# FNet mixing gated by a GLU: other places in the list of units, and an end in smaller pieces

## The chip, the cores and the metric

The kernel runs on one core of a Trainium2 chip. The time is the device time of one execution in microseconds (us); several executions are timed and their median is given. One further execution is recorded by the profiler, and everything that is read from a view of the profile comes from that one. The engines are TensorE (PE, matmuls), VectorE (DVE), ScalarE (ACT), GpSimd (POOL, which here only issues DMAs) and SyncE (SP, which issues loads and the last stores).

## The reference

x has 2048 rows and 512 columns; all matrices are float32.

```python
xn = layernorm(x)                                  # no scale, no offset
a, b = xn @ dft_hid_re.T, xn @ dft_hid_im.T        # DFT over the hidden dimension
s = dft_seq_re @ a - dft_seq_im @ b                # DFT over the sequence, real part
h = sigmoid(xn @ w_gate) * (xn @ w_up)             # GLU
g = silu(h @ w_down)
out = x + s * g
```

## The kernel before, in words

**Precision.** Each float32 operand is split into two parts by `split` (L70 to L73): a ScalarE copy rounded to the matmul's type (L72, "hi") and a VectorE subtraction that keeps the rest (L73, "lo"). `mm3` (L75 to L78) makes three matmuls of each product: hi by hi (L76), hi by lo (L77), lo by hi (L78). So the first matmul of a product needs only the copy, and the second the subtraction too.

**Fewer products.** All large products use a scheme of seven block products (numbered 1 to 7 in the code) instead of eight. Their operands are sums and differences of blocks, made by `combine` (L126 to L128) on VectorE; the results are put together from PSUM by copies on ScalarE (`snap`) and additions on VectorE (`plus`, `join`, `give`). The sequence DFT also uses its symmetry, which leaves some small products, here called inner products (letters a to g in a plan).

**Storage.** Working memory is a pool of pages of 512 KB. Which page a tile gets is settled when the program is built: one that is free by then in program order. The instruction that takes it waits on the chip until the page's last reader is done, and that reader can be a store. Partial results go to DRAM and come back: `g_part` (GLU output, L312, accumulated by the DMA), `f_part` (sequence DFT, L831), `s_part` (sums of xn, L647), `w_part` (differences of the hidden DFT's weights, L678), `i_part` (the inner products' operands, already split, `keep` in `inner_a`, L744). `put_x` copies x to the output (L979), onto which the gated blocks are accumulated at the end (L1032).

**The list of units.** A unit is one group of matmuls of some products and the operands that they need; `units` holds 251 of them, in this order:

- 0 to 90: thirteen GLU blocks of seven units, 18 matmuls each (4.1 us). Each takes one "down" product of an earlier block along (bank pd), whose result `gather` (L310 copies, L312 accumulate) brings out.
- 91 to 223: the sequence products of four chunks, 12 matmuls each (2.7 us). The order within a chunk is a string in `PLAN`: a digit is one of the four quarters of that block product, a letter an inner product (6 matmuls). The last down products (6 matmuls) are put in after so many digits (`LEFT`).
- 224 to 250: the hidden DFT, in two halves (pairs) of the output; the last unit is cut (`run_last`).

There is no scheduler. Before unit n the loop below emits what was registered for it by `sooner`, the loads of five units ahead and the splits of two units ahead (three, where n is in `deep`); then the matmuls; then what was registered by `after`. The engines work strictly in this order, so an instruction that waits holds back all behind it on its engine.

```python
for f in early.get(n, []):                                   # sooner(n, f)
    f()
for k in range(n, min(n + LOAD_AHEAD + 1, len(units))):      # loads, SP
    ...
for k in range(n, min(n + SPLIT_AHEAD + 1 + (n in deep), len(units))):   # splits, ACT and DVE
    ...
run()                                                        # matmuls, then copies out of PSUM
for f in extra.get(n, []):                                   # after(n, f)
    f()
```

The places are numbers in tables: `DEEP` (units with one more split ahead), `AL` (first operands made so many units early), a fixed 3 and 4 for the sums of a chunk and of the inner products, `SI`, `SL` and `GL` (silu, sums and splits of the hidden DFT), and a list for each of the inner operands, the weight differences and the copies of x.

Of the kernel before, what the change touches and what calls it, by code (L numbers as in the profile page):

```python
# [34 lines left out]
def fnet_glu_kernel(ctx: ExitStack, tc: tile.TileContext, x, x_t, c_re, c_im, w_h, w_gu, w_down, out):  # L35
# [285 lines left out]
    LEFT = 2,4,6,8,10,12,14  # L321
    HEAD = {(1, 0): "g", (1, 1): "g n u0", (2, 0): "u2", (2, 1): "p1 d0 d1 u1 r", (3, 0): "p3 x1 g d2 u3", (3, 1): "X5 g x2"}
    S0 = 7, 10, 11, 12
    H0 = 8, 12, 13, 14
    L4 = 9, 11, 14, 17
    S4 = 7,8,10,11
# [105 lines left out]
    def block(h, w, made, before, job, late):  # L432
# [3 lines left out]
        if not made:  # L436
            for i, v in zip((-3, 0, 1, 3), w["s"]):
                sooner(n + i, v.get)
# [255 lines left out]
    def a_operands():  # L694
# [11 lines left out]
        "1111 5555 6666 aa 3333 7777 bb 4444",  # L706
        "1e1e1f1f 5c5c55 66663g3g 7777 3d3d 4444",
        "11115555 6666aa7777bb4444 3e3e3f3f",
        "cc1g1g1d1d 5555 6666 33 7777 33 4444",
    )  # L710
    LETTER = "aabb"
    DEEP = {(c, k, 3) for c in range(2) for k in (1, 5, 6, 7, 4)}
    AL = {(0,4,0):4,(0,4,2):4,(0,7,0):4,(0,7,2):4,(0,3,0):4,(0,3,2):4}
# [68 lines left out]
    class Chunk:  # L782
# [102 lines left out]
    class Inner:  # L885
# [30 lines left out]
        def step(self, k):  # L916
            i, m = self.count[k], len(units)
            self.count[k] += 1
            if ("t", k, i) in self.b:
                v = self.b["t", k, i]  # L920
                sooner(m - 7, v.load)
                sooner(m - 4, v.get)
# [3 lines left out]
    def seq_units(job, c_sums):  # L926
# [4 lines left out]
        for q in range(2):  # L931
            sooner(n - 9 + 4 * q, ops[1, q].load)
            sooner(n - 5 + 4 * q, ops[1, q].get)
        inner_a([n + i for i in (-43,-41,-38,-36,-34,-31,-27,-24,-20,-6,-3)])
# [20 lines left out]
        sums_ahead(diffs, blocks, w_part, range(starts[2] + 5, starts[2] + 9), 4)  # L955


    def hidden_units():
# [4 lines left out]
        WH = {1: n - 11, 5: n - 8, 6: n - 5}  # L963
# [7 lines left out]
        LAST = NT // 2 - 1, 4  # L971
# [16 lines left out]
        SI = {(0,2):8,(0,7):9,(0,3):10}  # L988
        SL = {(0,6,0):4,(0,6,1):5,(0,7,0):5,(0,7,1):6}
        GL = {(0,5,0):3,(0,5,1):3,(0,6,0):3,(0,6,1):3,(0,2,0):3,(0,2,1):3,(0,7,0):3}  # L990
        for pair in range(NT // 2):
# [16 lines left out]
            for i, k in enumerate(TURNED):  # L1008
                if k in BLOCK and (pair, k) != LAST:
                    after(n - 88 + 4 * (i + 2 * pair), lambda pair=pair, k=k: put_x(pair, *BLOCK[k]))  # L1010
# [7 lines left out]
            def done(k, pair=pair, gl=gl, ps=ps, s=s, begin_chain=begin_chain):  # L1018
# [5 lines left out]
                def give(ch, name=None, op=None, swap=False):  # L1024
                    g = gl[BLOCK[k]].get()
                    r = s[name] if name else page([2, SB], F32)
                    for d in range(2):
                        a, b = r[:, d, :] if name else g[:, d, :], ps[ch, d]
                        nc.vector.tensor_tensor(r[:, d, :], *((b, a) if swap else (a, b)), op=op or ALU.mult)
                    if name:  # L1030
                        nc.vector.tensor_mul(r, r, g)
                    nc.gpsimd.dma_start(place_out(pair, *BLOCK[k]), r, accum_op=ADD)  # L1032
# [175 lines left out]
```

## Time and profile before

| what | before |
|---|---|
| median of 3 executions | 804.94 us (804.63 to 805.74) |
| the profiled execution | 803.52 us, of which the span is 801.7 us |
| matmuls, busy TensorE | 3588, 793.1 us |
| VectorE busy | 709.1 us, 928 instructions |
| ScalarE busy | 540.9 us |
| granted TensorE clock | 1.00 |

The span is what the profiler records from the first to the last instruction or transfer; 1.8 us of the execution lie around it. A matmul's end is modelled: one of 128x512 is shown with 0.39 us, while the next begins 0.23 us after it, so what TensorE loses is read from the starts of its matmuls and not from its busy time. A line such as "L72 ACT ACTIVATE page<-page" names the source line, the engine, the operation, and what is written and read, without the numbers of the buffers. What stands in brackets at a row's end is how long the engine was idle before it, and what ended that.

### The profile page before, as it was taken

The numbers are of one execution on the slowest core, as the hardware profiler recorded it, in microseconds if no ns is written. First come the engines' busy times: TensorE is split into PE (matmuls) and PEld (weight loads), VectorE is DVE, ScalarE is ACT, GpSimd is POOL, SyncE is SP. The second block draws the span as 40 slices with busy tenths as digits, with TensorE's granted clock in tenths as the row PEclk, the third lists the DMA queues.
The fourth block names the chain that finished last, engine by engine and source line by source line (L and its number), as shares of the span: only waits on it lengthen the run. The fifth ranks groups of instructions, "written<-read, shape, count | busy, mean of one in ns | idle before, by whom it ended". The sixth has DMA issues, their size and how long they took to land.

```text
span 801.7 us, 10262 instructions
## 1 busy us (share of the span) xinstructions
PE 793.1 (99%) x3588; PEld 656.1 (82%) x3588; DVE 709.1 (88%) x928; ACT 540.9 (67%) x840; POOL 122.0 (15%) x168
## 2 busy tenths in 40 slices
PE   9999999999999999999999999999999999999997
PEld 8988888888888888788888888788887888888886
DVE  7999889889998989988998897899698899888986
ACT  4688887888877878777977755553544645548371
POOL 2004351211221212121110000001010000000201
PEclk9999999999999999999999999999999999999999
DMA  7048799886986899987997797629977584874826
GB/s 282 35 158 209 175 222 207 210 159 106 182 206 217 218 232 261 252 204 149 243 325 221 194 346 229 210 80 331 410 264 260 200 303 185 301 269 164 206 57 106
DMA packets 49556, 172.13 MB, mean 215 GB/s; under 512 B 5472, under 2 KB 5728, under 8 KB 49504
## 3 DMA queue, kind: packets, MB, share of 16 engines
q0 software_dynamic: 20112, 69.75, 40.0%
q1 hardware_dynamic: 29312, 101.66, 36.0%
q8 instruction: 28, 0.46, 0.2%
q14 instruction: 24, 0.20, 0.1%
q10 hardware_dynamic: 80, 0.07, 0.0%
HBM read 104.86 MB, written 70.26 MB: 218 GB/s over the span
## 4 chain that ended last, share of the span: by engine, by line
PE 91%; issue 3%; DMA 3%; DVE 2%; ACT 0%; POOL 0%; ACTq 0%; DVEq 0%; POOLq 0%
PE pd L78 5%; PE pd L76 5%; PE pd L77 5%; PE ga L76 5%; PE ga L77 5%; PE ga L78 5%; PE ua L77 5%; PE ua L78 5%; PE ua L76 5%; PE gb L77 4%; PE gb L78 4%; PE gb L76 4%; PE gc L77 3%; PE gc L78 3%; PE ub L76 3%; PE uc L76 3%
## 5 line engine op out<-in xcount | busy, mean ns | idle before, releaser
L73 DVE TENSOR_TENSOR page<-page 128x1024 fp32r<-128x1024 f32 (+2 forms) x408 | 374.4, 944 | 64.1 <-ACT page L72 63.3
L72 ACT ACTIVATE page<-page 128x1024 fp32r<-128x1024 f32 (+2 forms) x408 | 319.1, 834 | 121.8 <-DVE page L128 109.8
L128 DVE TENSOR_TENSOR page<-page 128x512 f32<-128x512 f32 (+2 forms) x280 | 224.0, 819 | 1.2 <-DMA page<-in_w_gu_dram 0.3
L310 ACT ACTIVATE page<-pd 128x512 f32<-128x512 f32 x140 | 82.3, 600 | 44.5 <-PE pd L78 39.5
L312 POOL DMA_DIRECT2D g_part<-page x76 | 65.0, 855 | 277.0 <-ACT page L310 265.6
L76 PE MATMUL ga<-page 128*128 128x512 f32 x200 | 78.1, 390 | 0.5 <-ACT page L443 0.5
L77 PE MATMUL ga<-page 128*128 128x512 f32 x200 | 78.0, 390 | 0.0
L78 PE MATMUL pd<-page 128*128 128x512 f32 x200 | 77.9, 390 | 0.0
L78 PE MATMUL ga<-page 128*128 128x512 f32 x200 | 77.8, 389 | 0.0
L76 PE MATMUL pd<-page 128*128 128x512 f32 x200 | 77.8, 389 | 0.0
L77 PE MATMUL pd<-page 128*128 128x512 f32 x200 | 77.8, 389 | 0.0
L77 PE MATMUL ua<-page 128*128 128x512 f32 x196 | 76.4, 390 | 0.1
L76 PE MATMUL ua<-page 128*128 128x512 f32 x196 | 76.3, 389 | 0.0
L78 PE MATMUL ua<-page 128*128 128x512 f32 x196 | 76.3, 389 | 0.0
L77 PE MATMUL gb<-page 128*128 128x512 f32 (+1 forms) x140 | 53.8, 385 | 0.1
L78 PE MATMUL gb<-page 128*128 128x512 f32 (+1 forms) x140 | 53.6, 383 | 0.0
L76 PE MATMUL gb<-page 128*128 128x512 f32 (+1 forms) x140 | 53.6, 383 | 0.0
L77 PE MATMUL ub<-page 128*128 128x512 f32 x132 | 51.5, 390 | 0.0
L76 PE MATMUL ub<-page 128*128 128x512 f32 x132 | 51.4, 389 | 0.0
L78 PE MATMUL ub<-page 128*128 128x512 f32 x132 | 51.3, 389 | 0.0
L77 PE MATMUL gc<-page 128*128 128x512 f32 x124 | 48.9, 395 | 0.6 <-DVE page L73 0.5
L78 PE MATMUL gc<-page 128*128 128x512 f32 x124 | 48.4, 391 | 0.1
(154 smaller groups left out, 1296.1 us busy)
## 6 DMA issues: line engine op xcount, KB each, us to landing
g_part<-page POOLq DMA_DIRECT2D x84, 512.0 KB, 6.6
page<-in_c_re_dram SPq DMA_DIRECT2D x49, 512.0 KB, 5.2
page<-in_c_im_dram SPq DMA_DIRECT2D x33, 512.0 KB, 6.3
page<-in_w_gu_dram SPq DMA_DIRECT2D x26, 512.0 KB, 6.0
f_part<-page POOLq DMA_DIRECT2D x16, 512.0 KB, 4.9
page<-f_part SPq DMA_DIRECT2D x16, 512.0 KB, 3.7
page<-i_part SPq DMA_DIRECT2D x14, 512.0 KB, 4.2
page<-in_w_down_dram SPq DMA_DIRECT2D x13, 512.0 KB, 4.8
```

Source lines behind the costliest of these rows:

```text
L72: nc.scalar.activation(hi, src, AF.Copy)
L73: nc.vector.tensor_tensor(lo, src, hi.bitcast(F32), op=SUB)
L76: nc.tensor.matmul(ps, ws[0], ms[0], start=first, stop=False, skip_group_check=go_on)
L77: nc.tensor.matmul(ps, ws[0], ms[1], start=False, stop=False, skip_group_check=go_on)
L78: nc.tensor.matmul(ps, ws[1], ms[0], start=False, stop=last, skip_group_check=go_on)
L128: (engine or nc.vector).tensor_tensor(dst, a, b, op=op)
L310: nc.scalar.activation(pg[:, o, :], po, AF.Copy, scale=float(sign))
L312: nc.gpsimd.dma_start(g_part[i], pg, accum_op=ADD)
```

## The change

Nothing is computed in another way; the same products are made. Four things move, and the end is cut differently.

1. **Order of products.** Four strings of `PLAN` place the inner products (and a few quarters) elsewhere among the quarters, and `LEFT` brings the last two down products of a chunk one quarter earlier.
2. **Splits and sums of the chunks.** `DEEP` names other units. Two new tables, `CSUM` and `ISUM`, give the lead of single sums instead of the fixed 3 and 4 units. `AL` makes some first operands 3 to 6 units early.
3. **Other operands.** The inner operands (`inner_a`, sums, splits and their stores by POOL), the weight differences (units 164, 170, 173 and 178 instead of 167 to 170), the sums of xn and x, the silu calls, sums and splits of the hidden DFT, the copies of x by POOL, and the operands of the GLU blocks (`S0`, `H0`, `L4`, `S4`, `w["s"]`) get other places.
4. **The end.** The last but one block of output is gated and accumulated in two halves of 256 KB instead of one of 512 KB. The last unit makes its two halves in pieces of 256, 320, 256 and 192 columns instead of 256, 512 and 256; the final store, on two queues, is 192 columns wide instead of 256.

```diff
-    LEFT = 2,4,6,8,10,12,14
+    LEFT = 2, 4, 6, 8, 10, 11, 13
...
-        "1e1e1f1f 5c5c55 66663g3g 7777 3d3d 4444",
+        "11ee1f15fc5c5566663gg377773d3d4444",
...
-    DEEP = {(c, k, 3) for c in range(2) for k in (1, 5, 6, 7, 4)}
+    DEEP = {(0, 1, 3), (0, 5, 3), (0, 6, 3), (0, 7, 3), (0, 4, 3), (1, 1, 3), (1, 5, 3), (1, 7, 3), (1, 4, 3), (3, 6, 3), (2, 4, 0), (2, 6, 3), (3, 4, 1), (3, 7, 3), (0, 7, 1), (3, 7, 0), (2, 7, 2), (0, 6, 0)}
+    CSUM = {(0, 7, 1): 5, (2, 6, 0): 4, (2, 6, 1): 5, (1, 6, 0): 2, (3, 4, 2): 3, (1, 5, 1): 5, (2, 6, 3): 3}
...
                 v = self.sums[k, pp]
-                sooner(m - 6, v.load)
-                sooner(m - 3, v.get)
+                lead = CSUM.get((self.tc, k, pp), 3)
+                sooner(m - lead - 3, v.load)
+                sooner(m - lead, v.get)
...
-        inner_a([n + i for i in (-43,-41,-38,-36,-34,-31,-27,-24,-20,-6,-3)])
+        inner_a([n + i for i in (-45, -38, -37, -36, -34, -31, -27, -24, -16, -10, -4)])
...
-        sums_ahead(diffs, blocks, w_part, range(starts[2] + 5, starts[2] + 9), 4)
+        sums_ahead(diffs, blocks, w_part, [starts[2] + i for i in (2, 8, 11, 16)], 4)
...
                 def give(ch, name=None, op=None, swap=False):
                     g = gl[BLOCK[k]].get()
                     r = s[name] if name else page([2, SB], F32)
+                    halves = (pair, k) == (LAST[0], 3)
                     for d in range(2):
                         a, b = r[:, d, :] if name else g[:, d, :], ps[ch, d]
                         nc.vector.tensor_tensor(r[:, d, :], *((b, a) if swap else (a, b)), op=op or ALU.mult)
+                        if halves:
+                            nc.vector.tensor_mul(r[:, d, :], r[:, d, :], g[:, d, :])
+                            nc.gpsimd.dma_start(place_out(pair, *BLOCK[k])[:, d, :], r[:, d, :], accum_op=ADD)
+                    if halves:
+                        return
...
-                for d, at in ((0, slice(0, SB // 2)), (1, slice(0, SB)), (0, slice(SB // 2, SB))):
+                for d, at in ((0, slice(0, SB // 2)), (1, slice(0, CUT)), (0, slice(SB // 2, SB)), (1, slice(CUT, SB))):
```

(`CUT` is 320. Line numbers after the change are 2 to 11 higher than before: L807, L814 and L824 become L809, L816 and L826, and L744 becomes L746.)

How this moves single instructions is shown at three places. First POOL near the end of the GLU blocks, at unit 71 to 78; each row is one DMA, written tensor and read page. Before:

```order
L312 DMA g_part5_91<-page_3316 128x1024
L744 DMA i_part_96<-page_3324 128x1024
L312 DMA g_part7_93<-page_3360 128x1024
L312 DMA g_part6_92<-page_3400 128x1024
L312 DMA g_part4_90<-page_3472 128x1024
```

And after:

```order
L312 DMA g_part5_91<-page_3316 128x1024
L312 DMA g_part7_93<-page_3355 128x1024
L312 DMA g_part6_92<-page_3393 128x1024
L312 DMA g_part4_90<-page_3466 128x1024
L746 DMA i_part_96<-page_3475 128x1024
```

The store of the fifth inner operand stood behind unit 71's accumulate and now stands behind unit 75's.

Second ScalarE at units 107 to 112: L72 are hi copies, L807 (L809) the copy of a finished block product, L310 the copy of a down product. Before:

```order
L72 ACTIVATE page_4372<-page_4311 128x1024
L72 ACTIVATE page_4376<-page_4333 128x1024
L807 ACTIVATE page_4392<-ga_4064 128x512
L807 ACTIVATE page_4392<-ua_4065 128x512
L310 ACTIVATE page_4401<-pd_4218 128x512
L310 ACTIVATE page_4401<-pd_4219 128x512
L72 ACTIVATE page_4407<-page_4349 128x1024
L72 ACTIVATE page_4418<-page_4370 128x1024
L72 ACTIVATE page_4422<-page_4190 128x1024
```

And after:

```order
L72 ACTIVATE page_4372<-page_4318 128x1024
L310 ACTIVATE page_4382<-pd_4220 128x512
L310 ACTIVATE page_4382<-pd_4221 128x512
L72 ACTIVATE page_4386<-page_4337 128x1024
L72 ACTIVATE page_4390<-page_4339 128x1024
L72 ACTIVATE page_4394<-page_4354 128x1024
L809 ACTIVATE page_4410<-ga_4064 128x512
L809 ACTIVATE page_4410<-ua_4065 128x512
L72 ACTIVATE page_4422<-page_4019 128x512
L912 ACTIVATE ub_4431<-gb_4415 128x512
L72 ACTIVATE page_4433<-page_4190 128x1024
L72 ACTIVATE page_4449<-page_4413 128x1024
```

The down product and its copies stand ahead of the block product's; the split for unit 111 (page_4407 before, page_4394 after) stood behind all four copies and now stands between the two pairs, with those for units 114 and 110.

Third VectorE at units 179 to 182: L814 (L816) is the join of a finished product with a copied one, L128 a sum for a later operand, L73 a lo subtraction. Before:

```order
L73 TENSOR_TENSOR page_5686<-page_5628,page_5685 128x1024
L814 TENSOR_TENSOR page_5518<-gb_5352,page_5518 128x512
L814 TENSOR_TENSOR page_5518<-ub_5353,page_5518 128x512
L128 TENSOR_TENSOR page_5266<-page_5266,page_5646 128x1024
L73 TENSOR_TENSOR page_5708<-page_5251,page_5707 128x1024
L128 TENSOR_TENSOR page_5284<-page_5284,page_5664 128x1024
```

And after:

```order
L128 TENSOR_TENSOR page_5266<-page_5266,page_5630 128x1024
L816 TENSOR_TENSOR page_5514<-gb_5355,page_5514 128x512
L816 TENSOR_TENSOR page_5514<-ub_5356,page_5514 128x512
L73 TENSOR_TENSOR page_5708<-page_5266,page_5707 128x1024
L128 TENSOR_TENSOR page_5284<-page_5284,page_5661 128x1024
L73 TENSOR_TENSOR page_5721<-page_5663,page_5720 128x1024
```

The sum in page_5266 stood behind the two joins and now stands ahead of them; only one subtraction (page_5708, for unit 182) comes directly behind the joins.

More of the change, by code (lines that the diff above doesn't have):

```diff
@@ L920, in step @@
                 v = self.b["t", k, i]
[L921 to L922 removed]
+                lead = ISUM.get((self.one.tc, k, i), 4)
+                sooner(m - lead - 3, v.load)
+                sooner(m - lead, v.get)
             add([self.a[k], self.b[k, i]], lambda: self.run(k, i))
```

50 lines of the change are left out of this document (26 added, 24 removed).

## The prediction

> **What bounds the kernel now.** I read the page's first part (busy time), then the part on the chain that ended last, then TensorE in stretches of 20 us.
>
> ```profile
> PE 793.1 (99%) x3588; PEld 656.1 (82%) x3588; DVE 709.1 (88%) x928; ACT 540.9 (67%) x840; POOL 122.0 (15%) x168
> PE 91%; issue 3%; DMA 3%; DVE 2%; ACT 0%; POOL 0%; ACTq 0%; DVEq 0%; POOLq 0%
> ```
>
> TensorE carries the chain. How much a better order can win is what TensorE waits. In the next view each row is 20 us: the stretch, its length, TensorE's busy time with the matmuls that touch it, the granted clock, the DMA share and GB/s. The stretches run on without a gap from 40 us; the first row is a full one, and of the 37 up to 780 us these ten have fewer than 90 from 320 us on.
>
> ```profile
> 40.00:60.00 20.00, 20.00 (x90) 1.00 0.46 158
> ...
> 320.00:340.00 20.00, 19.46 (x86) 1.00 1.04 253
> ...
> 440.00:460.00 20.00, 20.00 (x89) 1.00 0.73 188
> 460.00:480.00 20.00, 20.00 (x89) 1.00 0.97 339
> 480.00:500.00 20.00, 19.99 (x89) 1.00 0.71 231
> 500.00:520.00 20.00, 19.39 (x83) 1.00 0.70 215
> ...
> 600.00:620.00 20.00, 19.89 (x87) 1.00 0.74 259
> ...
> 640.00:660.00 20.00, 19.89 (x88) 1.00 0.84 295
> 660.00:680.00 20.00, 20.00 (x88) 1.00 0.51 189
> ...
> 720.00:740.00 20.00, 19.95 (x88) 1.00 0.54 184
> 740.00:760.00 20.00, 20.00 (x89) 1.00 0.82 200
> ```
>
> The clock is 1.00 throughout. In the full row about 88.2 starts fall into 20 us (two of the 90 only reach in), so a 128x512 matmul costs 0.2267 us. The ten rows lack 4+1+1+1+7+3+2+2+2+1 = 24 starts: 24 x 0.2267 = 5.4 us. This, and the tail after the last matmul, is all that a new order can win. The Trainium skill, "Perfetto Trace Analysis", section "Identifying the Most-Contended Engine", holds matmul busy share for a poor measure of headroom and takes the weight loads' share instead; by that the 82% above would leave 18% or some 144 us. The trace does not bear this out here: the rows show a constant start-to-start time with 5.4 us of holes, so the sum goes by holes.
>
> **The change part by part.** A unit is one group of matmuls; every operand is split into hi (ScalarE copy, L72) and lo (VectorE subtraction, L73), two units ahead, on engines that work strictly in the written order. Each hole has something late ahead of such a split. I go through them in order of time; the numbers of units count from 0.
>
> *Unit 74 (337 us).* Columns from here: start, length, engine, operation, and in brackets idle time and its releaser.
>
> ```profile
> 330.10 0.56 POOL L744 DMA_DIRECT2D i_part<-page  x1 [2.23 <-DVE page L73]
> ...
> 337.56 0.60 ACT L443 ACTIVATE page<-ga 128x512 f32<-128x512 f32 x1 [2.21 <-DMA i_part<-page]
> ...
> 337.29 0.39 PE L78 MATMUL pd<-page 128*128 128x512 f32 x1
> 338.21 0.50 PE L76 MATMUL ga<-page 128*128 128x512 f32 x1 [0.54 <-ACT page L443]
> ```
>
> ScalarE's copy of the finished product (L443) takes the page that a store of an inner operand frees: issued 330.10, landed just before 337.56. TensorE needs that bank and starts at 338.21 instead of 337.29+0.23 = 337.52. The change moves this store from unit 71 to 75, so the copy no longer waits; ScalarE had idled 2.21 us before it, and would then be bound by the copy's own matmuls. The rows lack 4 starts (0.91 us); I take -0.8. What is late next: the split for unit 80, issued at unit 78, now takes that page; a landing of again 7.4 us ends before TensorE comes to it by some 3 us, as the store leaves POOL about 4 units (16 us) later and 5 units ahead of unit 80 (20 us).
>
> *Units 108 to 111 (447 us).*
>
> ```profile
> 442.66 0.60 ACT L807 ACTIVATE page<-ga 128x512 f32<-128x512 f32 x1 [0.80 <-PE ga L78]
> ...
> 444.08 1.22 ACT L310 ACTIVATE page<-pd 128x512 f32<-128x512 f32 x2
> 445.19 2.94 ACT L72 ACTIVATE page<-page 128x1024 fp32r<-128x1024 f32 x3
> ...
> 446.28 3.50 DVE L73 TENSOR_TENSOR page<-page 128x1024 fp32r<-128x1024 f32 x3 [2.78 <-ACT page L72]
> ...
> 447.22 0.39 PE L76 MATMUL gc<-page 128*128 128x512 f32 x1
> ```
>
> Four copies out of PSUM that wait for TensorE stand ahead of the split for unit 111 (which starts at 447.22), and VectorE idles 2.78 us. After the change all three splits stand ahead of L807: -0.25 (one start lacking). Its cost: the s_part load for unit 116 is issued by SP only after the last matmul of unit 108 (about 444.7 us, when the second copy of the L310 row begins), and on ScalarE the split for 114 stands behind the split that needs it. At 5.3 us, the first row below, it lands at 450.0; two copies and, on VectorE, two subtractions and the sum now placed between them, at 1.14 us each, end at 454.5. Unit 114 comes 30 matmuls after 447.22 and, with the hole, at 454.3, its second matmul, which needs the subtraction, at 454.5; without the hole 0.25 sooner. Nothing hides more than that. Lower bound 0, upper bound from the second row, 10.3 - 5.3 = 5.0 us; I take +0.2, nearest to the row of the same place.
>
> ```profile
> page<-s_part SPq DMA_DIRECT2D x3, 512.0 KB, 5.3
> ...
> page<-s_part SPq DMA_DIRECT2D x2, 512.0 KB, 10.3
> ```
>
> The first is of 438 to 453 us, the second of 404 to 421 us, when the DMA engines were full.
>
> *Units 123 to 126 (476 to 485 us).* Two starts (0.45). The moved a-operand splits stand ahead of the join and free some 0.15; the rest is the copy between two chunks, which is not moved: -0.15.
>
> *Units 128 to 140 (500 to 520 us): the largest.*
>
> ```profile
> 494.00 0.91 POOL L312 DMA_DIRECT2D g_part<-page  x1 [7.99 <-ACT page L310]
> 504.68 0.87 POOL L312 DMA_DIRECT2D g_part<-page  x1 [9.78 <-ACT page L310]
> ...
> 501.87 1.06 ACT L72 ACTIVATE page<-page 128x1024 fp32r<-128x1024 f32 x1 [2.79 <-DMA g_part<-page]
> ...
> 512.45 1.23 DVE L73 TENSOR_TENSOR page<-page 128x1024 fp32r<-128x1024 f32 x1 [0.25 <-DMA g_part<-page]
> ...
> 513.73 0.50 PE L77 MATMUL gc<-page 128*128 128x512 f32 x1 [0.47 <-DVE page L73]
> ```
>
> Seven starts, 1.6 us. Two accumulates into g_part (7.9 and 7.7 us to landing) hold the pages that the splits for units 136 and 140 take. With the down product at unit 128 instead of 129 the first accumulate leaves 1.4 us (six matmuls) sooner, its page goes to a later subtraction, and the sums for 135 and 136 stand earlier: I take away three of the four waits, 1.2 us. The second accumulate stays at unit 134 and its page stays with unit 140: that 0.4 us (513.73 instead of 513.10, with what the late first step adds) is kept.
>
> *Units 176, 182, 195, 205/206 (600 to 670 us).*
>
> ```profile
> 614.06 0.69 DVE L814 TENSOR_TENSOR page<-gb,page 128x512 f32<-128x512 f32 x1 [1.21 <-PE gb L78]
> ...
> 615.35 1.22 DVE L128 TENSOR_TENSOR page<-page 128x1024 f32<-128x1024 f32 x1
> 616.48 1.22 DVE L73 TENSOR_TENSOR page<-page 128x1024 fp32r<-128x1024 f32 x1
> ...
> 617.75 0.50 PE L77 MATMUL gb<-page 128*128 128x512 f32 x1
> ```
>
> This is unit 182. VectorE waits 1.21 us for a product to end (join, L814), and sum and subtraction come behind it; the subtraction ends at 617.70, 0.2 after it was due. After the change the sum stands ahead of the join, into the 1.21 us of idleness: the subtraction ends 1.14 us earlier, with a margin of some 0.9 us. The other three places are of the same kind and get the same cure (one extra unit of lead for a split or a sum). The rows lack 3+2+2 = 7 starts, 1.6 us; I take -1.4.
>
> *Unit 230 (736 us).* Two starts (0.45). Silu calls on ScalarE stand between splits; one goes four units later and one sum earlier: -0.3. The one start at 740 to 760 us is left.
>
> Moved without a price: the weight differences (units 164 to 178 instead of 167 to 170), their loads, the x-to-out copies and the sums in the GLU part. They lie where the rows have 90 starts, TensorE's cover there being two units of finished splits, 5.4 us and more; if the cover goes, each late split costs one VectorE step, 1.14 us. For these and for new narrow places I put +0.3 (from 0 to 1.5).
>
> **The end.**
>
> ```profile
> 796.11 0.42 DVE L1072 TENSOR_TENSOR page<-page,gb 128x256 f32<-128x256 f32 x1
> ...
> out_dram<-page POOLq DMA_DIRECT2D x2, 512.0 KB, 6.2
> out_dram<-page SPq DMA_DIRECT2D x1, 256.0 KB, 4.1
> out_dram<-page SPq DMA_DIRECT2D x1, 128.0 KB, 1.9
> out_dram<-page SPq DMA_DIRECT2D x1, 64.0 KB, 3.4
> ```
>
> Twelve matmuls of 512 columns become twelve of 320 and twelve of 192. By column that is nothing; if a 192 costs as much as half a 512 it is 12 x (0.142+0.113-0.227) = +0.35; I take +0.15. VectorE's last pair is shorter (192 instead of 256 columns): -0.1. The last store took 3.4 us beside one of 256 KB issued 0.9 us earlier, while 128 KB alone took 1.9. The new one has 48 KB per queue and follows 128 KB; between 0 and -1.5 I take -0.45, since the last 512 KB accumulate (6.2 us from 793.39, so 799.6) would otherwise end last, and its two halves carry the same bytes. Tail: -0.4 (from +0.4 to -0.9).
>
> Sum: -0.8 -0.25 +0.2 -0.15 -1.2 -1.4 -0.3 +0.3 -0.4 = -4.0 us. The profiled execution took 803.52 (span 801.7 and 1.8 around it) and would take 799.5. It lay 1.4 below the median of the runs, 804.94; against that I predict 800.9. Its own range: 799.3 to 803.
>
> **Rivals.** *The holes only move* (the change doesn't do what it says): VectorE is 88% busy, and what stands earlier pushes something else. It speaks for this that every cure is a reordering with the same work; against it, that VectorE idles 1.2 to 2.8 us right at the holes. If the places win half and lose as much, 804.9.
>
> *Slower: the s_part load for unit 116.* It is the only price above that has no cover: each us that it lands after 5.3 us goes into the end, since ScalarE stands still on it, and the split for unit 114 behind it. From 9.3 us on nothing is left of the gain, from 10.9 us on the kernel is slower; at 11.1 us, as a c_im load of the same size had it in the full stretch, it is 5.8 - 0.2 - 4.0 = +1.6, so 806.5.
>
> ```profile
> page<-in_c_im_dram SPq DMA_DIRECT2D x3, 512.0 KB, 11.1
> ```
>
> For it: the change also moves two loads and an accumulate at units 105 to 107 close ahead. Against it: DMA share 0.73 in that row, beside 1.04 at 400 to 420 us.
>
> *The tail gets longer.* If the two 256 KB halves of the last accumulate don't overlap but follow one another, each with the 1.9 us that even a small store takes, the end comes 1.9 us after 799.6 rather than at 800.0, so +1.5 on the forecast: 802.4. The Trainium skill, "DMA: Bandwidth & Descriptors", section "Anatomy of one DMA — SWDGE (gpsimd) path", gives each transfer on this path about 2.0 us that do not scale with size, which speaks for a price of smaller pieces; the 1.9 us row agrees.
>
> **How the numbers follow.** Chances: the forecast 0.60, holes only move 0.13, slow load 0.16, long tail 0.11. A measurement here tells about 0.2% (1.6 us) from no change. Faster (below 803.3): 0.60 and 0.11, 0.71; same 0.13; slower (over 806.5) 0.16. The range 799.0 to 805.8 takes in the long tail and the moved holes, and leaves out the slow load and a little below.
>
> **What would show it.** In the stretches of 20 us: 90 starts at 320 to 340 and 600 to 680, at least 87 at 500 to 520. No releaser i_part for L443 and none g_part for L72. The L814 joins (then L816) behind the sums. Last store under 3 us. Wrong it would be if 440 to 460 lacks more than two starts, if new rows below 90 appear at 560 to 600 (loads of 10 us there), or if the split for unit 80 waits for the moved store.

## The result, and the profile after

| | before | after |
|---|---|---|
| median of 9 executions | 804.94 us (803.45 to 807.84) | 800.88 us (799.84 to 803.59) |
| ratio of the times | | 0.9958, 95% interval 0.9946 to 0.9969 |
| profiled execution, its span | 803.52, 801.7 us | 799.84, 798.1 us |

By the medians the changed kernel is 4.1 us faster, by the ratio 3.4 us (2.5 to 4.3). The first part of the page of after, and then TensorE in the same stretches of 20 us as in the prediction (length, busy time and matmuls, clock, DMA share, GB/s):

```profile
PE 790.9 (99%) x3600; PEld 657.7 (82%) x3600; DVE 710.4 (89%) x931; ACT 540.2 (68%) x840; POOL 123.7 (16%) x169
```

```profile
320.00:340.00 20.00, 20.00 (x90) 1.00 1.06 251
...
440.00:460.00 20.00, 20.00 (x90) 1.00 0.73 180
460.00:480.00 20.00, 18.98 (x84) 1.00 0.90 303
480.00:500.00 20.00, 19.99 (x87) 1.00 0.80 248
500.00:520.00 20.00, 20.00 (x90) 1.00 0.68 221
...
600.00:620.00 20.00, 20.00 (x89) 1.00 0.95 331
...
640.00:660.00 20.00, 20.00 (x90) 1.00 0.84 303
660.00:680.00 20.00, 20.00 (x90) 1.00 0.50 162
...
720.00:740.00 20.00, 20.00 (x90) 1.00 0.70 237
740.00:760.00 20.00, 20.00 (x89) 1.00 0.83 181
```

The ten rows lacked 24 starts before; now they lack 6+3+1+1 = 11. Thirteen starts of 0.2267 us are 2.9 us. Most holes are gone, but 460 to 480 us, which lacked one start, lacks six, and 480 to 500 us three instead of one. Where the larger new hole lies, in the timelines of POOL, ScalarE, VectorE and TensorE (start, length, engine, operation, idle time and its releaser):

```profile
460.65 0.56 POOL L833 DMA_DIRECT2D f_part<-page  x1 [7.64 <-DVE page L816]
...
468.24 2.01 ACT L72 ACTIVATE page<-page 128x1024 fp32r<-128x1024 f32 x2 [2.37 <-DMA f_part<-page]
...
469.33 2.36 DVE L73 TENSOR_TENSOR page<-page 128x1024 fp32r<-128x1024 f32 x2 [1.89 <-ACT page L72]
471.61 0.68 DVE L816 TENSOR_TENSOR page<-ga,page 128x512 f32<-128x512 f32 x1
...
471.04 0.39 PE L78 MATMUL ub<-page 128*128 128x512 f32 x1
472.44 0.47 PE L76 MATMUL ga<-page 128*128 128x512 f32 x1 [1.02 <-DVE page L816]
```

A store of f_part, issued at 460.65, holds a page; the split for unit 121 takes that page and waits 2.37 us; two subtractions come after it on VectorE, and only then the join (L816) that empties the banks ga and ua. Unit 121 writes into these banks. The new order of products leaves one inner product between (six matmuls), where before there were two, and TensorE stands 1.2 us. Before the change the same store landed after 4.3 us instead of 7.6, and no split waited for it.

Put together from the starts of TensorE's matmuls in the two traces:

| part | before | after | difference |
|---|---|---|---|
| start of the span to the first GLU product | 34.18 | 34.62 | +0.43 |
| first product to the first matmul of the last unit | 756.12 | 753.09 | -3.03 |
| last unit, first to last matmul | 5.49 | 5.84 | +0.35 |
| last matmul's start to the end of the span | 5.96 | 4.52 | -1.44 |
| span | 801.75 | 798.06 | -3.69 |

In what follows "middle" is the second of these rows, and a hole is what lies between two starts of matmuls beyond 0.2267 us.

### The profile page after: what moved, and what is told of

It reads as the page before. It is cut to its first block, busy times and chain, and to the rows that moved or that the text cites. A ratio compares the mean times of both kernels' runs of the same rounds, so it can differ in the third digit from the quotient of the medians.

```text
span 798.1 us, 10300 instructions
## 1 busy us (share of the span) xinstructions
PE 790.9 (99%) x3600; PEld 657.7 (82%) x3600; DVE 710.4 (89%) x931; ACT 540.2 (68%) x840; POOL 123.7 (16%) x169
## 4 chain that ended last, share of the span: by engine, by line
PE 96%; DMA 2%; DVE 1%; issue 0%; ACT 0%; DVEq 0%
PE pd L78 6%; PE pd L76 6%; PE pd L77 6%; PE ga L76 6%; PE ga L77 5%; PE ga L78 5%; PE ua L76 5%; PE ua L77 5%; PE ua L78 5%; PE gb L76 4%; PE gb L77 4%; PE gb L78 4%; PE ub L78 4%; PE ub L77 4%; PE ub L76 4%; PE gc L78 3%
## 5 line engine op out<-in xcount | busy, mean ns | idle before, releaser
L73 DVE TENSOR_TENSOR page<-page 128x1024 fp32r<-128x1024 f32 (+2 forms) x408 | 373.9, 943 | 61.4 <-ACT page L72 60.7
L72 ACT ACTIVATE page<-page 128x1024 fp32r<-128x1024 f32 (+2 forms) x408 | 317.5, 832 | 116.3 <-DVE page L128 105.5
L128 DVE TENSOR_TENSOR page<-page 128x512 f32<-128x512 f32 (+2 forms) x280 | 223.1, 817 | 0.9
L310 ACT ACTIVATE page<-pd 128x512 f32<-128x512 f32 x140 | 82.1, 600 | 41.8 <-PE pd L78 38.5
L77 PE MATMUL ub<-page 128*128 128x512 f32 (+2 forms) x136 | 52.1, 383 | 0.0
L78 PE MATMUL ub<-page 128*128 128x512 f32 (+2 forms) x136 | 52.1, 383 | 0.0
L76 PE MATMUL ub<-page 128*128 128x512 f32 (+2 forms) x136 | 52.1, 383 | 0.0
```

The source lines that it names most:

```text
L72: nc.scalar.activation(hi, src, AF.Copy)
L73: nc.vector.tensor_tensor(lo, src, hi.bitcast(F32), op=SUB)
L76: nc.tensor.matmul(ps, ws[0], ms[0], start=first, stop=False, skip_group_check=go_on)
L77: nc.tensor.matmul(ps, ws[0], ms[1], start=False, stop=False, skip_group_check=go_on)
L78: nc.tensor.matmul(ps, ws[1], ms[0], start=False, stop=last, skip_group_check=go_on)
L128: (engine or nc.vector).tensor_tensor(dst, a, b, op=op)
```

## Experiments

Each has one profiled execution; three were also timed over several executions beside the kernel before.

### Which of its two causes makes the new hole

`e1_bb` gives back the old order at the end of chunk 0, so that two inner products lie between.

```diff
-        "111155556666aa33337777b4b444",
+        "111155556666aa33337777bb4444",
```

> The changed kernel, with the order of products of chunk 0 ending 7777 bb 4444 as before instead of 7777 b4b444. Theory: the one new hole, 1.2 us at 472 us, comes about because only one inner product (six matmuls, 1.36 us) lies between the last matmul into the banks ga and ua and their next use, while the join that empties them stands on VectorE behind subtractions that wait for a store of f_part. With both inner products between, there are 2.7 us, and the hole at 471 to 473 goes: the stretch 460 to 480 us has 89 or 90 starts instead of 84, the span falls from 798.1 to about 796.9 (start of the first product equal). Rival: the join is late by more than that wherever it stands (the store lands late); then the hole stays over 0.5 us.

Measured: no hole at 472 us. The median is 799.91 us of 5 (ratio to before 0.9937, 0.9924 to 0.9950). The span of the profiled execution was 798.7, not 796.9: its first product began at 35.85 us instead of 34.62, and holes of 0.3 us stood at 455 and 504 us. The middle was 752.45, 0.6 less than the changed kernel. But in this run no split waited for the store of f_part either: it landed after 4.80 us. So the hole went while both of its conditions were gone, and whether two inner products would hide the wait isn't tried.

`e2_al` leaves the order of products and takes the wait away, by making one operand earlier, as before the change.

```diff
-    AL = {(0, 4, 2): 6, ...}
+    AL = {(0, 4, 0): 4, (0, 4, 2): 6, ...}
```

> The changed kernel, with the first operand of product 4 (first half) in chunk 0 split four units early again, as before the change; the order of products stays as changed. Theory: the hole at 472 us needs both the short distance and the wait of the split for unit 121 on the page of the f_part store (ScalarE idle 2.37 us). With the split made earlier that page goes to the split for unit 122, the join comes one subtraction (1.14 us) sooner, and the hole shrinks from 1.2 to at most 0.2 us; span about 797.0. Rival: the short distance between the two uses of the bank alone makes the hole; then it stays at 1.2 us and the stretch 460 to 480 us keeps 84 starts.

```profile
460.00:480.00 20.00, 20.00 (x90) 1.00 0.93 327
...
469.62 0.68 DVE L816 TENSOR_TENSOR page<-ga,page 128x512 f32<-128x512 f32 x1
```

These are the stretch and the join in `e2_al`: the join begins at 469.62 instead of 471.61, and TensorE has 90 starts. The middle is 751.86, 1.23 less, the median 799.55 of 4 (ratio 0.9936, 0.9919 to 0.9953). So the short distance alone does not make this hole; it takes the page's wait ahead of the join as well. What took the wait away is not separated: the operand takes its page earlier, and the store also landed sooner, after 4.61 us.

The other runs of this document, described below, have the same place. Their store of f_part (issue to landing), the wait of the split behind it, and the hole at 472 us:

| run | store | wait | hole |
|---|---|---|---|
| `e11_plan1` | 8.58 | 3.52 | 2.41 |
| `e6_end_old` | 7.66 | 2.58 | 1.48 |
| after | 7.57 | 2.37 | 1.26 |
| `e7_one_acc` | 7.54 | 2.47 | 1.37 |
| `e9_load_slow` | 7.43 | 2.33 | 1.22 |
| `e13_load_slow` | 5.85 | 0.78 | 0 |
| `e4_sums_old`, `e10_plan_old`, `e5_left_old` | 4.92, 4.90, 4.83 | none | 0.23, 0.37, 0.08 |
| `e1_bb`, `e2_al`, `e12_best` | 4.80, 4.61, 4.57 | none | 0 |

With the short distance the hole is the wait less 1.1 us, five times out of five, and none where the wait was 0.8 us. Without a wait up to 0.4 us is left in three kernels; in them the join follows nine subtractions on VectorE without a pause. Two inner products instead of one would be 1.36 us more between the two uses of the bank, about as much as the hole of after: that is an estimate from six matmuls of 0.2267 us.

### One number of the change alone: the store behind unit 75

```diff
-        inner_a([n + i for i in (-43,-41,-38,-36,-34,-31,-27,-24,-20,-6,-3)])
+        inner_a([n + i for i in (-43,-41,-38,-36,-34,-31,-27,-24,-16,-6,-3)])
```

> The kernel before, with one number changed: the fifth inner operand is split and stored behind unit 75 instead of 71. Theory: the page of this store alone made the hole at 337 to 339 us; it goes, 320 to 340 us has 90 starts instead of 86, span about 800.9 instead of 801.7; all other holes stay. Rival: the copy L443 only took the page that happened to be late, and the next store in line (g_part, 8 us to landing) takes its place: the hole stays over 0.5 us.

```profile
320.00:340.00 20.00, 20.00 (x90) 1.00 1.03 242
...
500.00:520.00 20.00, 18.69 (x79) 1.00 0.71 212
```

The hole at 338 us went, as expected; but the span is 802.0 and the middle 756.21, as before the change (756.12). The stretch at 500 to 520 us lacks 11 starts where it had lacked 7. What was won is given back there: ScalarE's split for unit 136 waits 4.06 us on the page of the g_part accumulate where it had waited 2.79.

```profile
493.46 0.90 POOL L312 DMA_DIRECT2D g_part<-page  x1 [8.16 <-ACT page L310]
...
502.43 1.06 ACT L72 ACTIVATE page<-page 128x1024 fp32r<-128x1024 f32 x1 [4.06 <-DMA g_part<-page]
```

The accumulate left 0.54 us earlier than before the change, and the split could start 0.56 us later: it took 1.1 us longer, and nothing in the edit touches it. One execution can't say how often that happens, so whether the gain is lost as a rule stays open.

### The tables of sums, and the strings

`e4_sums_old` undoes the new places of sums and splits in the changed kernel: `DEEP` as before, `CSUM` and `ISUM` empty.

```diff
-    DEEP = {(0, 1, 3), (0, 5, 3), ...}
-    CSUM = {(0, 7, 1): 5, ...}
-    ISUM = {(2, 5, 1): 5, ...}
+    DEEP = {(c, k, 3) for c in range(2) for k in (1, 5, 6, 7, 4)}
+    CSUM = {}
+    ISUM = {}
```

> The changed kernel with DEEP of before and without CSUM and ISUM (every sum 3 or 4 units ahead). Theory: the holes of units 176, 182, 195 and 205/206 come back, because sums and splits stand behind joins and copies again: 600 to 680 us lacks 5 to 8 starts, 1.2 to 1.8 us, and the span is 799.3 to 800.2. Rival: these holes went because the weight differences and their loads left 580 to 592 us free; then 600 to 680 us keeps at most one start lacking and the span stays within 0.4 us of 798.1.

```profile
600.00:620.00 20.00, 19.87 (x88) 1.00 0.91 321
...
640.00:660.00 20.00, 20.00 (x90) 1.00 0.84 297
660.00:680.00 20.00, 20.00 (x89) 1.00 0.51 171
```

Three starts are lacking, not five to eight. A hole of 0.37 us stands at 614 us, but not the old one: it lies ahead of the first matmul of its unit, which starts 0.15 us after the join that empties the bank gb has ended (614.17), where before the change the second matmul stood behind a subtraction. The other three holes stay away, so they did not need the tables. The middle is 752.76, 0.33 less than with them (753.09): small holes came (0.22 at 366 us, 0.24 more at 614), and the one at 472 us fell to 0.23. `e10_plan_old` also puts back the strings of chunks 2 and 3:

```diff
-        "111155556666a7a777b44b443e3e3f3f",
-        "1ccg1g1d155d556666337777334444",
+        "11115555 6666aa7777bb4444 3e3e3f3f",
+        "cc1g1g1d1d 5555 6666 33 7777 33 4444",
```

> The previous run's kernel (changed kernel with the old lead of every sum and the old set of deep units) with also the order of products of chunks 2 and 3 as before the change. Theory: the holes of units 182, 195 and 205/206 were cured by these two strings, which put an inner product between two quarters where a join stands on VectorE; with the old strings they return: 600 to 680 us lacks 4 to 7 starts, 0.9 to 1.4 us of holes at 617, 646 and 667 to 670 us, and the span rises by about as much. Rival: the weight differences (spread over 14 units instead of 4) cured them; then at most 0.4 us of holes returns there.

```profile
600.00:620.00 20.00, 19.89 (x88) 1.00 0.91 329
...
640.00:660.00 20.00, 19.89 (x88) 1.00 0.87 299
660.00:680.00 20.00, 20.00 (x88) 1.00 0.48 163
```

Six starts are lacking, and the holes stand where they stood before the change, with the same sizes: 0.22 (602 us), 0.38 (616), 0.38 (645), 0.21 and 0.11 (666 and 669), 1.3 us together. The weight differences stayed spread in this run, so they had no part in it. The two strings are enough to cure these holes, but for the 0.37 us at 614. Whether the new tables with the old strings would be enough too isn't tried.

`e5_left_old` and `e11_plan1` were to do the same for the holes of 500 to 520 us.

```diff
-    LEFT = 2, 4, 6, 8, 10, 11, 13
+    LEFT = 2, 4, 6, 8, 10, 12, 14
```

> The changed kernel with the last two down products of each chunk behind the 12th and 14th quarter as before, not the 11th and 13th. Theory: the accumulate into g_part then leaves later and its page is again late for the splits behind it: the stretch 500 to 520 us loses 2 to 5 of its 90 starts (0.5 to 1.2 us), and 440 to 460 us loses one. Rival: the new order of inner products in chunk 1 alone keeps TensorE fed there; then 500 to 520 us keeps 89 or 90.

```profile
440.00:460.00 20.00, 19.49 (x87) 1.00 0.69 163
...
500.00:520.00 20.00, 20.00 (x90) 1.00 0.70 218
```

With the old places of the down products 500 to 520 us stays full, but a hole of 0.78 us comes at 448 us, where TensorE waited 0.2 to 0.3 before the change. So the earlier down product pays at units 108 to 111. About 500 to 520 us this run says nothing: the 11th and the 13th quarter of `LEFT` are reached in chunk 0 alone, where seven down products are left, and chunk 1 takes its two behind the 2nd and the 4th quarter in both versions. The first accumulate of chunk 1 leaves at the same time in after and in `e5_left_old`:

```profile
493.00 0.91 POOL L312 DMA_DIRECT2D g_part<-page  x1 [6.43 <-ACT page L310]
...
493.00 0.90 POOL L312 DMA_DIRECT2D g_part<-page  x1 [6.45 <-ACT page L310]
```

What moved its down product from unit 129 to 128 is the string of chunk 1: with 11ee the second quarter is over six matmuls sooner than with 1e1e. (The middle of `e5_left_old` is 753.08, as with the change: the hole at 472 us was 0.08 in this run.)

```diff
-        "11ee1f15fc5c5566663gg377773d3d4444",
+        "1e1e1f1f 5c5c55 66663g3g 7777 3d3d 4444",
```

> The changed kernel with the order of products of chunk 1 as before (1e1e1f1f 5c5c55 ...), all else as changed, the earlier down products too. Theory, after the run with the old down products had 90 starts at 500 to 520 us: it is this string that cured the holes of units 128 to 140; with the old one 500 to 520 us lacks 3 to 7 starts (0.7 to 1.6 us). Rival: either of the two, string or down products, is enough, or the other moved splits are; then 500 to 520 us keeps 89 or 90.

```profile
460.00:480.00 20.00, 17.83 (x79) 1.00 0.85 308
...
500.00:520.00 20.00, 19.12 (x84) 1.00 0.78 235
...
496.35 0.91 POOL L312 DMA_DIRECT2D g_part<-page  x1 [7.82 <-ACT page L310]
...
503.41 1.06 ACT L72 ACTIVATE page<-page 128x1024 fp32r<-128x1024 f32 x1 [1.99 <-DMA g_part<-page]
...
514.28 2.36 DVE L73 TENSOR_TENSOR page<-page 128x1024 fp32r<-128x1024 f32 x2 [1.01 <-DMA g_part<-page]
```

With the old string of chunk 1 six starts are lacking at 500 to 520 us. The first accumulate leaves six matmuls later again, and a split waits 1.99 us for its page, as before the change; but that wait costs TensorE nothing here, for there is no hole from 500 to 514 us. The missing starts are one hole of 1.15 us at 514 us, where a subtraction waits for the page of the second accumulate. Its down product ends at the same place in the order as in after, and it landed after 7.9 us here, 6.8 there. So the run shows that the string moves the first accumulate and its wait; that the string alone cured the holes it doesn't show.

The hole at 472 to 475 us also grows, to 2.4 us. The middle is 756.12, as in the kernel before: of the 3.0 us these two holes take back 2.3, and holes of 0.55 us at 334 and 0.33 at 454 us the rest, with the one at 494 us gone.

### The end

`e6_end_old` is the changed kernel with the old end, `e7_one_acc` undoes only the two halves of the accumulate.

```diff
-                    halves = (pair, k) == (LAST[0], 3)
+                    halves = False
```

(in both), and in `e6_end_old` also

```diff
-                for d, at in ((0, slice(0, SB // 2)), (1, slice(0, CUT)), (0, slice(SB // 2, SB)), (1, slice(CUT, SB))):
+                for d, at in ((0, slice(0, SB // 2)), (1, slice(0, SB)), (0, slice(SB // 2, SB))):
```

> The changed kernel with the end of before: one accumulate of 512 KB for the last but one block, and the last unit in 256, 512 and 256 columns. The first theory (from the two traces): the last unit's matmuls take 0.35 us less (5.49 instead of 5.84), and from the last matmul to the end of the span it is 5.9 instead of 4.5 us; together +1.1 us, span 799.2 if the hole at 472 us is as long. Rival: the shorter end comes from where the loads and stores of the blocks before happen to lie and not from the pieces; then the time behind the last matmul stays within 0.4 of 4.5 us.

> The changed kernel with one accumulate of 512 KB for the last but one block instead of two of 256 KB; the last unit in four pieces as changed. If the columns of the last pieces make the end shorter (less in flight when the last store is issued), the time behind the last matmul stays 4.4 to 4.8 us and the span 798.1. If the halves make it (the accumulate is done earlier), it rises to 5.3 us or more.

| | before | old end | one accumulate | after |
|---|---|---|---|---|
| last unit, first to last matmul | 5.49 | 5.49 | 5.84 | 5.84 |
| last matmul's start to the end | 5.96 | 5.48 | 4.99 | 4.52 |
| sum | 11.45 | 10.97 | 10.83 | 10.36 |

The halves are worth 0.47 us, the cut at 320 columns 0.49 behind the last matmul and 0.35 against it: both parts help, the new end by 0.6 us against the old one under the same kernel. Neither expectation of `e7_one_acc` was met: 4.99 lies between its two, since each part brings about half. The 5.48 of `e6_end_old` lies between its two as well (5.9, or 4.9 at most). The old end itself stood at 5.96 and 5.93 (`e3_store75`) with the old order and at 5.48 with the new one, while the ten profiles that have the whole new end lie between 4.51 and 4.54. So 0.5 us of the 1.1 us between the two profiles goes with the rest of the change and not with the pieces; what in it does this isn't tried. In `e7_one_acc` and then in after, the DMAs of the end (KB each, us to landing):

```profile
out_dram<-page SPq DMA_DIRECT2D x1, 160.0 KB, 4.7
out_dram<-page SPq DMA_DIRECT2D x1, 48.0 KB, 2.6
```

```profile
out_dram<-page POOLq DMA_DIRECT2D x1, 512.0 KB, 6.2
out_dram<-page POOLq DMA_DIRECT2D x2, 256.0 KB, 4.4
out_dram<-page SPq DMA_DIRECT2D x1, 160.0 KB, 2.5
out_dram<-page SPq DMA_DIRECT2D x1, 48.0 KB, 2.1
```

With the accumulate in halves the stores beside it land sooner. Half the bytes take 4.4 us instead of 6.2 (for another block, earlier).

### The price of a late s_part load

The load for unit 116 was the rival on the slower side. The table below gives its time in six executions, from SP's issue to the start of the copy that waits for it, and the hole at 454 us. `e9_load_slow` was to slow the load, but its edit changed two entries of a table that no block uses; it is the changed kernel once more.

> The changed kernel with the first two copies of x to the output (512 KB each, issued by POOL) behind units 105 and 106 instead of 147 and 152, so that they run beside the s_part load for unit 116, issued at 444 us. Theory: nothing covers this load. In the runs so far it took 4.7 to 5.3 us, and the hole at 454 us was 0 at 4.7 and 4.8, 0.3 at 5.1 and 0.5 at 5.3. If it lands after L us, the hole is L - 4.8 us: 3 us for a load of 8 us, and the span longer by that. Rival: ScalarE and VectorE catch up over the units between; then the hole is less than half of L - 4.8.

`e13_load_slow` moves the two copies that were meant.

```diff
-                    after(n - (88, 84, 79, 77, 72, 67, ...)[i + 6 * pair], ...)
+                    after(n - (88, 84, 79, 119, 118, 67, ...)[i + 6 * pair], ...)
```

> The changed kernel with its first two copies of x to the output (blocks 2 and 7 of the first half) behind units 105 and 106 instead of 147 and 152, so that they run beside the s_part load for unit 116, issued at 444 us. (The earlier run of this name changed two entries that no block uses, so that it was the changed kernel once more: there the load took 5.3 us and the hole was 0.46 us, as on the line below.) Theory: nothing covers this load, and the hole at 454 us is its landing time less 4.8 us: 3.2 us for a landing after 8 us; the span grows by that. Rival: ScalarE and VectorE catch up; then the hole is less than half of the landing time less 4.8 us.

```profile
443.98 3.07 SPq L87 DMA_DIRECT2D page<-s_part  x2
...
450.86 2.01 ACT L72 ACTIVATE page<-page 128x1024 fp32r<-128x1024 f32 x2 [2.59 <-DMA page<-s_part]
...
455.50 0.50 PE L77 MATMUL gc<-page 128*128 128x512 f32 x1 [1.79 <-DVE page L73]
```

| execution | issue | copy starts | load | hole |
|---|---|---|---|---|
| after | 444.22 | 448.89 | 4.67 | 0 |
| `e2_al` | 444.20 | 449.01 | 4.81 | 0 |
| `e7_one_acc` | 444.13 | 449.21 | 5.08 | 0.27 |
| `e9_load_slow` | 444.23 | 449.52 | 5.29 | 0.46 |
| `e6_end_old` | 444.55 | 449.85 | 5.30 | 0.48 |
| `e13_load_slow` | 443.98 | 450.86 | 6.88 | 2.06 |

The hole is the load's time less 4.8 us in every row: nothing covers it. `e1_bb` and `e11_plan1` fit in (5.12 and 5.17 us, holes of 0.30 and 0.33). `e4_sums_old` and `e10_plan_old`, with the old tables, don't: at 5.04 and 5.16 us they have no hole, so it is the new places of sums and splits that leave this load uncovered. But the kernel of `e13_load_slow` did not get longer by its hole. The middle of `e13_load_slow` is 753.99, that of `e9_load_slow`, the same kernel with the load on time, 753.96. Of the 1.6 us more at 454 us 1.2 are given back at 472: no hole there in `e13_load_slow`, 1.22 us in `e9_load_slow`. The store of f_part was issued 1.3 us later and yet landed 0.2 us sooner, at 468.5, so the split hardly waited for it. That is one execution; where the hole at 454 us was 0.27 to 0.48, the one at 472 was no smaller than in after (1.37, 1.22 and 1.48 against 1.26).

### All three places mended

`e12_best` is the changed kernel with the edit of `e2_al`, the operand of unit 116 one unit later (behind the split for 114), and the splits for unit 131 one unit earlier.

```diff
-    AL = {(0, 4, 2): 6, (0, 7, 0): 4, ...}
+    AL = {(0, 4, 0): 4, (0, 4, 2): 6, (0, 7, 0): 3, ...}
...
         chunks = [Chunk(i, c_sums) for i in range(NT)]
+        deep.add(n + 37)
```

> The changed kernel with three edits: the first operand of product 4 in chunk 0 split four units early again (the run that took away the hole at 472 us), the operand of unit 116 one unit later, behind the split for unit 114 (so that the s_part load holds back nothing that is due), and the splits for unit 131 one unit earlier, ahead of the copies of the down product. Theory: the holes at 454, 472 and 494 us go in every execution; holes of 0.5 to 0.7 us are left (484, 614 and 749 us), the span is 796.3 to 797.0, the median 798.6 to 799.4, about 0.7% under the kernel before. Rival: each moved split pushes another one late, and 0.3 us or more of new holes appears between 440 and 520 us.

```profile
440.00:460.00 20.00, 20.00 (x90) 1.00 0.79 185
460.00:480.00 20.00, 20.00 (x90) 1.00 0.90 319
480.00:500.00 20.00, 19.99 (x89) 1.00 0.79 253
500.00:520.00 20.00, 20.00 (x90) 1.00 0.68 215
```

The median is 798.49 us of 5 (798.23 to 799.13), ratio to before 0.9925 (0.9911 to 0.9939): the fastest of all. Holes of 0.7 us are left: 0.18 at 334, 0.28 at 484, 0.13 at 614 and 0.11 at 749 us.

## Why the prediction was right, and where it wasn't

The time (800.9 predicted, 800.88 measured) came out closer than its terms did: two of them missed, in opposite directions, and one had the right size with a cure that was wrong in part. That the two numbers agree to 0.02 us is luck: the two profiled executions differ by 3.7 us where -4.0 was forecast, and nine executions of the changed kernel lie up to 3.8 us apart. The right column is the difference between the starts of the same matmul (counted from the first product) ahead of and behind each place.

| term | predicted | the two traces |
|---|---|---|
| unit 74 | -0.8 | -0.84 |
| units 108 to 111, with the s_part load | -0.05 | -0.25 |
| units 123 to 126 | -0.15 | -0.2 |
| units 128 to 140 (500 to 520 us) | -1.2 | -1.6 |
| units 176 to 206 | -1.4 | -1.3 |
| unit 230 | -0.3 | -0.35 |
| new narrow places | +0.3 | +1.3 (at 472 us), +0.25 (at 494 us) |
| the end | -0.4 | -1.1 |
| the start | none | +0.4 |

The right column sums to -3.7, which is what the spans differ by. Of the signs that the prediction named, most came: 90 starts at 500 to 520 us and at 560 to 600, no releaser i_part for L443, a last store of 2.1 us. L72 no longer waits for g_part at 500 to 520 us, though it does at 325, 332 and 368 (2.5 us together), and 600 to 620 us has 89 starts and not 90.

**The bound.** That only holes and the end can be won held: the start-to-start time is 0.2267 us in both traces, and the middle fell by 3.0 us, where the terms for it summed to -3.6.

**Unit 74.** Right in place, cause and size; `e3_store75` removes this hole by the one number. That its gain goes into the time was not seen when it was made alone: the next page wait, at 502 us, ends when a transfer lands, and that transfer took 1.1 us longer in the one execution.

**Units 108 to 111.** Right, and the condition on the s_part load was right too: at 5.3 us the prediction put 0.2 us, and 0.46 and 0.48 were measured; in the profiled execution of after it took 4.67 and cost nothing.

**Units 128 to 140.** The size was near (-1.2 against -1.6). The step "with the down product at unit 128 instead of 129 the first accumulate leaves" 1.4 us sooner held: it leaves six matmuls earlier, at 493.00 instead of 494.00 us, and no split of these units waits for a page of g_part in after. It is the string of chunk 1 that moves it and not `LEFT`. What the first three waits need is not separated: with the old string the wait comes back but not their holes, and with the new string and the old tables (`e4_sums_old`) there are none either. The 0.4 us that were to stay at unit 140 are gone in after, but 0.11, 0.26 and 0.34 us stand there, at 513 us, in three more executions of the same instructions; so that term was about right, and after fell out well.

**Units 176 to 206.** Again the size was right and the named cure wrong in part. A sum did leave its place behind the joins, but "one extra unit of lead for a split or a sum" is not what that takes: without these tables three of the four holes stay away, and with the old strings as well all four return, to a hundredth of a microsecond. That the order of products sets which operand is due behind a join, and so the sum's place, is how I read it; the new tables with the old strings were not run.

**New narrow places.** The term that missed most: +1.55 against +0.3, just past its bound of 1.5. The prediction looked for late splits and took TensorE's cover to be two units of finished splits. At 472 us what is late is not an operand but a bank of PSUM: the join has to read it before the next product of that chunk begins, and that distance was halved. The 0.25 us at 494 us look like the price of the earlier down product: they are there in every run with the new string of chunk 1 except `e12_best`, which puts the splits for unit 131 ahead of its copies, and not in `e11_plan1`.

**The end.** -1.1 against -0.4. The matmuls cost +0.35, the upper of the two prices given: twelve of 192 columns, from 792.33 to 793.54, take 0.110 us each, hardly less than one of 256 (0.119). Of the -1.44 behind them the pieces explain 0.96 by `e6_end_old` and `e7_one_acc`; 0.5 goes with the rest of the change. The Trainium skill, "DMA: Bandwidth & Descriptors", section "Anatomy of one DMA — SWDGE (gpsimd) path", puts about 2.0 us that don't scale with size on each transfer on POOL's path and moves the bytes at 436 GB/s. By that half of 512 KB would save 0.6 us, which is an estimate from the page's figure. Here the accumulate went from 6.2 to 4.4 us, 1.8 us less, three times as much; two sizes, with the halves in flight together, don't show whether it is the size alone.

**The start.** +0.43 us was in no term. The first product began between 34.2 and 35.9 us in the fourteen profiled executions, at 34.2 and 34.3 in the two with the old order in the GLU part, at 34.3 to 35.9 in the twelve others. Whether the change has a part in that stays open.

**The rivals.** *The holes only move* came true at 472 us, and for the store behind unit 75 when it was moved alone, in one execution. *The slow load* was right as a mechanism, one for one, though the hole at 5.3 us was 0.46 and 0.48 instead of 0.2. Its price, each us into the end, fits the executions with small holes there and not `e13_load_slow`, where the next hole gave most of it back; no load came near the 9.3 us from which nothing would be left. (By its own rule, each us beyond 5.3 on top of -4.0, a load of 11.1 us makes +1.8 and not +1.6.) *The longer tail* did not occur: the halves save 0.47 us. They overlap: issued at 788.31 and 789.63, they land at 792.44 and 794.26, 3.8 us before the end. The 1.9 us row beside that rival is a store on SP's queue, not one of POOL's.

## What to carry to other kernels

Where an engine without gaps is fed by others in a fixed order, count the starts it lacks in equal stretches, and look at each hole; but holes are no independent terms: those that wait for a transfer's landing can grow when an earlier hole is taken away, and shrink when one opens. When the order of products is changed, check for each bank of PSUM how much work lies between its last matmul and its next use, and what stands ahead of the instruction that empties it. A store whose page is taken soon after is a wait in hiding: moving the operand behind it by two units took the wait away and was worth 1.2 us here, about as much as the two strings of chunks 2 and 3.

## What was not expected of the hardware

The same transfers land at different times from execution to execution. In after, `e6_end_old`, `e7_one_acc` and `e9_load_slow`, which issue the same instructions up to the last units, the s_part load took 4.67 to 5.30 us and the holes differ:

| hole at | after | old end | one accumulate | repeated |
|---|---|---|---|---|
| 334 us | 0 | 0.29 | 0 | 0 |
| 454 us | 0 | 0.48 | 0.27 | 0.46 |
| 472 us | 1.26 | 1.48 | 1.37 | 1.22 |
| 513 us | 0 | 0.34 | 0.11 | 0.26 |

Their middles are 753.09, 754.46, 753.59 and 753.96: up to 1.4 us between executions is such waiting. Where these holes are gone (`e12_best`), five executions lay within 0.9 us of one another, where nine of the changed kernel spread over 3.8 us. Waiting need not be all of that: the two longest of the nine, 803.08 and 803.59 us, are also the two with the lowest granted clock, 0.996 and 0.997 against 0.999 to 1.000 for the others and for `e12_best`, and where TensorE carries the time, 0.3% less clock would make 800 us 2.4 us longer, by an estimate. The other seven spread over 2.6 us.

The store of f_part that makes the hole at 472 us took 4.3 us before the change and 7.6 after it. In after the store's first packet moves at 464.4 us, 3.7 us behind its issue: SP had issued two loads of in_c_re_dram at 459.8 and 460.3, just ahead of it, and the first of them lands at 464.8. Before the change SP issued no load in the 5.0 us ahead of the store (issued at 462.2), and its packets move about 1 us behind its issue. So the loads ahead may hold it back, but no run tried it.
